# Where the last six scatters of list entries run in a mixture-of-experts kernel, and when slot 3's list is loaded

## The chip, the cores and the metric

The kernel runs on one core of one Trainium2 chip. The metric is the device time of one execution in microseconds. The kernel before took 495.93 us as the median of three runs (495.6 to 498.26 us).

The core has five engines, each with its own instruction queue: TensorE (PE in the profile: matmuls; PEld: its weight loads), VectorE (DVE), ScalarE (ACT), GpSimd (POOL) and SyncE (SP). They wait for each other through semaphores. SP issues the plain DMAs and POOL the indirect ones (gathers and scatters by a list of rows); both run on the core's 16 DMA engines.

## The reference

A windowed attention is followed by a mixture of experts, in which each token goes to one of eight experts. The part that matters here is the second:

```
logits = x @ w_gate                       # x: 3072 x 512, w_gate: 512 x 8
e_idx  = np.argmax(logits, axis=1)        # one expert for each token
gate_w = softmax(logits)[token, e_idx]
eom    = 1 / (1 + np.exp(-(x @ w_output_gate)))
for e in range(8):
    mask = e_idx == e
    h  = np.maximum(x[mask] @ w1[e], 0.0)         # 512 x 1024
    ye = h @ w2[e]                                # 1024 x 512
    out[mask] = gate_w[mask, None] * eom[mask, e, None] * ye
```

The attention has 4 batches of 768 tokens; x is its output.

## The kernel before

**Lists.** For each batch, `route` finds each token's expert and its place in that expert's list. The lists lie in DRAM (`l_dr`). An entry is 8 bytes: the token's row and its weight. A batch has 768 tokens, six for each of 128 partitions, so POOL writes its entries with six indirect DMAs of 128 entries each (line 629), each after a memset of one column of a small tile `gap` (line 628). These are the scatters. `route` is a generator; for the last batch `attention` hands out its last six steps as a list of functions, `scatters`, and each call issues one memset and one scatter.

**Slots.** The experts' work is cut into slots of 256 tokens of one expert. The first three (`EARLY = 3`: slots 0, 1 and 2) are filled from the first batches alone. Which expert and which part of its list slots 3 and up take is found by `rest_slots`, some twenty small steps on DVE, which need the last batch's counts. For a slot, `fetch_list` (line 872) reads the list's place into a register of SP, lets SP load the 256 entries (line 880) and makes this load wait for all scatters issued so far in the program; `fetch` lets POOL gather the 256 rows of x (line 893) into `xg`.

**A slot's work.** `take_x` transposes the gathered rows on TensorE (line 943), and ACT and DVE split them into a rounded part and a residue. The first product has eight steps (`first`, lines 980 to 982): 12 matmuls of 256 columns each into one of the four PSUM banks P, S, p, s in turn; ACT takes the rounded part of the result (`hh`, line 983), DVE the residue (`hl`, line 984). The second product has eight steps too (`second_block`, lines 1290 to 1292) of six matmuls of 512 columns, which accumulate in two further banks; step j needs `hh` and `hl` of step j. At the end DVE and ACT scale the result (lines 1319 and 1321), and POOL writes the rows to the output by an indirect DMA (line 1322).

**Weights.** SP loads weight tiles of 128x512 into a ring of raw tiles (line 923), and ACT (line 931) and DVE (line 932) split each into a rounded part and a residue, once the tile of the slot before is free. The weights of slots 1 and 2 are loaded by an own loop (`load_ahead`), called each time a raw tile is split (`split`).

**Order.** Up to the end of slot 1 the order on all engines is written out by hand: `attention` and then `full_with(1, ...)`, which is the function that is changed. It goes through slot 1's first product; after each step it takes up to three steps of `rest_slots`, splits up to one tile of weights and issues one scatter. Then come the eight steps of the second product, with `take_x` for slot 2 ahead of the third step; after a step, once the table of slots 3 and up is made, it calls `fetch_list(3)`; and it splits the remaining weights of slot 2. After it come the write of slot 1's rows, the gather for slot 3 and the load of slot 4's list. From slot 2 on (`run`) only POOL's order is fixed by hand; a planner orders the other engines.

Of the kernel before, what the change touches and what calls it, by code (L numbers as in the profile page):

```python
# [11 lines left out]
F32 = mybir.dt.float32  # L12
# [39 lines left out]
NF = F // P  # L52
SLOT = 256
EARLY = 3
# [212 lines left out]
def in_bank(ps, bank, shape, name):  # L267
    return ps.tile(shape, F32, name=name, tag=f"bank{BANKS.index(bank)}", bufs=1)
# [560 lines left out]
class Experts:  # L829
# [244 lines left out]
    def full_with(self, s, scatters, rest):  # L1074
        hidden = self.hidden()
        made = None
        for j in range(NF):
            self.first(j, hidden, None)
            self.free += 4 * (j % 4 == 3)
            for _ in range(REST):  # L1080
                made = made or next(rest, None)
            self.split(EARLY_V, "v")
            if scatters:
                scatters.pop(0)()
        yp = [in_bank(self.ps, "Vv"[t], [P, DM], f"yp{t}") for t in range(2)]
        for j in range(NF):
            if j == 2:
                self.take_x(2)
            self.second_block(j, yp, *hidden)
            self.free += 1  # L1090
            if not self.slots.get(EARLY):
                for _ in range(REST):
                    made = made or next(rest)
                if made:
                    self.add_slots(made[0])
                    self.fetch_list(EARLY, 2)
            self.split(-(-len(self.behind) // (NF - j)))
        self.write(s, yp)
        assert not self.behind and not scatters
        self.fetch(EARLY, 2)  # L1100
        self.fetch_list(EARLY + 1, 2)
        return made[1]
# [323 lines left out]
```

## Time and profile before

| what | value |
|---|---|
| median of three runs | 495.93 us |
| the profiled execution, its own time | 493.42 us |
| its span, from the first to the last instruction | 491.3 us |
| mean granted clock of TensorE | 0.99 |
| TensorE busy | 468.6 us (95% of the span) |
| DVE, ACT, POOL busy | 365.7, 315.4, 179.5 us (74%, 64%, 37%) |

The profile was taken from one execution. All times in it count from the first instruction. An engine is busy while it executes an instruction; in the timeline a number in brackets is the idle time before a row, with what ended it. PEclk is the clock that TensorE was granted, as a share of 2.4 GHz. The DMA share is the mean over the 16 DMA engines; it passes 1 in some stretches.

### The profile page before, as it was taken

What the parts mean: (1) busy time and instruction counts of PE and PEld (TensorE: products, weight loads), DVE (VectorE), ACT (ScalarE), POOL (GpSimd) and SP (SyncE); (2) the same over time, 40 slices, a digit from 0 to 9 for tenths busy, and PEclk for the clock granted to TensorE, in tenths of its full rate; (3) what the DMA queues carried; (4) which work ended last, traced back from release to release, by engine and by line L of the source; (5) the groups of instructions that cost most, each with busy time, mean ns of one, the idle gap of its engine ahead of it and who ended that gap; (6) DMA issues with size and microseconds to landing.
All of it is one profiled execution on the core that took longest, in us unless ns stands there. A gap on an engine that the chain in (4) does not pass through costs nothing. (4 is left out here: it accounts for less than half of the span.)

```text
span 491.3 us, 12041 instructions
## 1 busy us (share of the span) xinstructions
PE 468.6 (95%) x4060; PEld 379.8 (77%) x4060; DVE 365.7 (74%) x822; ACT 315.4 (64%) x647; POOL 179.5 (37%) x194
## 2 busy tenths in 40 slices
PE   9999999997699999799999999999999999999994
PEld 4757886875488776689888888888888888888873
DVE  4988899799388529695778878787878689879610
ACT  2586787986396336265676868686767579679500
POOL 2575784537574367603130021203122212303101
PEclk9999999999899999989999999999999999999998
DMA  9997997969194628829877485867675678874730
GB/s 240 218 189 174 280 224 188 264 126 249 53 333 139 193 86 296 328 80 355 264 223 267 138 291 160 288 191 273 179 270 187 220 240 282 314 239 139 242 143 13
DMA packets 109962, 105.33 MB, mean 214 GB/s; under 512 B 47929, under 2 KB 72891, under 8 KB 109884
## 3 DMA queue, kind: packets, MB, share of 16 engines
q1 hardware_dynamic: 104588, 91.78, 64.2%
q0 software_dynamic: 5296, 12.62, 7.0%
q8 instruction: 35, 0.57, 0.5%
q14 instruction: 43, 0.35, 0.2%
HBM read 93.08 MB, written 13.46 MB: 217 GB/s over the span
## 5 line engine op out<-in xcount | busy, mean ns | idle before, releaser
L932 DVE TENSOR_TENSOR w2l<-raw,w2h 128x512 fp32r<-128x512 f32 x101 | 70.5, 716 | 21.4 <-ACT w2h L931 20.2
L931 ACT ACTIVATE w2h<-raw 128x512 fp32r<-128x512 f32 x104 | 64.7, 630 | 26.8 <-PE yp L1292 19.3
L893 POOL DMA_INDIRECT xg<-x_dr,lst x30 | 35.9, 1195 | 124.3 <-PE xp L943 108.1
L932 DVE TENSOR_TENSOR w1l<-raw,w1h 128x512 fp32r<-128x512 f32 x99 | 66.2, 694 | 6.4 <-ACT w1h L931 2.9
L1290 PE MATMUL yp<-w2h,hh 128*128 128x512 f32 x176 | 70.5, 401 | 0.0
L1291 PE MATMUL yp<-w2l,hh 128*128 128x512 f32 x176 | 69.4, 394 | 0.0
L1292 PE MATMUL yp<-w2h,hl 128*128 128x512 f32 x176 | 68.7, 396 | 0.2
L1322 POOL DMA_INDIRECT out_dram<-y,lst x26 | 27.8, 1068 | 105.6 <-DVE y L1319 30.3
L931 ACT ACTIVATE w1h<-raw 128x512 fp32r<-128x512 f32 x104 | 62.1, 624 | 2.7 <-PE hp L969 1.5
L973 PE MATMUL hp<-xhl,w1h 128*128 128x512 f32 x216 | 62.1, 395 | 0.0
L478 POOL TENSOR_TENSOR pr<-pr,mn 128x960 f32<-128x960 f32 x24 | 43.7, 1824 | 27.1 <-DVE mn L473 10.4
L971 PEld LDWEIGHTS hp<-xhl,w1l 128*128 128x128 f32 x288 | 44.3, 189 | 5.9
L971 PE MATMUL hp<-xhl,w1l 128*128 128x256 f32 x288 | 46.1, 281 | 0.0
L983 ACT ACTIVATE hh<-hs 128x256 fp32r<-128x256 f32 x72 | 29.8, 413 | 17.8 <-DVE hs L976 14.2
L1292 PEld LDWEIGHTS yp<-w2h,hl 128*128 128x128 f32 x176 | 33.3, 190 | 8.1 <-DVE hl L1135 1.0
L984 DVE SCALAR_TENSOR_TENSOR hl<-hs,hh 128x256 fp32r<-128x256 f32 x72 | 30.3, 421 | 11.9 <-ACT hh L983 10.6
L1291 PEld LDWEIGHTS yp<-w2l,hh 128*128 128x128 f32 x176 | 33.5, 190 | 6.8
L1290 PEld LDWEIGHTS yp<-w2h,hh 128*128 128x128 f32 x176 | 33.4, 190 | 6.7
L973 PEld LDWEIGHTS hp<-xhl,w1h 128*128 128x128 f32 x216 | 35.8, 189 | 3.2
L976 DVE TENSOR_TENSOR hs<-hp,hs 128x256 f32<-128x256 f32 x72 | 30.3, 421 | 9.8 <-ACT hs L975 7.5
L975 ACT ACTIVATE hs<-hp 128x256 f32<-128x256 f32 x72 | 27.2, 378 | 13.9 <-PE hp L973 10.5
L466 DVE TENSOR_TENSOR pr<-sp,c_sb 128x480 f32<-128x480 f32 x48 | 28.9, 649 | 8.9 <-PE sp L456 5.6
(223 smaller groups left out, 962.0 us busy)
## 6 DMA issues: line engine op xcount, KB each, us to landing
raw<-in_moe_w_dram SPq DMA_DIRECT2D x224, 256.0 KB
raw_k<-in_k_dram SPq DMA_DIRECT2D x12, 512.0 KB
raw_q<-in_q_dram SPq DMA_DIRECT2D x12, 512.0 KB
x_dr<-xs SPq DMA_DIRECT2D x24, 256.0 KB
vw<-in_v_dram SPq DMA_DIRECT2D x44, 128.0 KB
vw<-in_v_dram SPq DMA_DIRECT2D x44, 64.0 KB
w1l<-in_moe_w_dram SPq DMA_DIRECT2D x8, 256.0 KB
w2l<-in_moe_w_dram SPq DMA_DIRECT2D x8, 256.0 KB
```

The lines of the kernel that those rows point to most:

```text
L478: nc.gpsimd.tensor_tensor(pr, pr, mns.pop(i).unsqueeze(2).to_broadcast([P, H, W]), ALU.subtract)
L893: nc.gpsimd.indirect_dma_start(out=self.xg[t], out_offset=None, in_=self.x_dr[0:rows, :], in_offset=bass.IndirectOffsetOnAxis(ap=self.list ...
L931: nc.scalar.activation(hi, raw, AF.Copy)
L932: (lo_by or nc.vector).tensor_tensor(lo, raw, hi.bitcast(F32), ALU.subtract)
L971: nc.tensor.matmul(hp[:, 0, :], lhsT=w_l[c], rhs=self.xh[:, c, :], start=False, stop=False)
L973: nc.tensor.matmul(hp, lhsT=w_h[c], rhs=self.xhl[:, c], start=False, stop=c == NC - 1)
L976: nc.vector.tensor_tensor(hs, hp[:, 0, :], hs, ALU.add)
L983: nc.scalar.activation(hh[:, j, :], hs, AF.Relu)
L984: nc.vector.scalar_tensor_tensor(hl[:, j, :], hs, 0.0, hh[:, j, :].bitcast(F32), ALU.max, ALU.subtract)
L1290: nc.tensor.matmul(y, lhsT=hh[:, j, tk], rhs=w_h, start=j == 0, stop=False)
L1291: nc.tensor.matmul(y, lhsT=hh[:, j, tk], rhs=w_l, start=False, stop=False)
L1292: nc.tensor.matmul(y, lhsT=hl[:, j, tk], rhs=w_h, start=False, stop=j == NF - 1)
```

## The change

The six scatters no longer stand in the loop over the first product. After that loop POOL copies one element column of the last step's residue (`hidden[1][:, NF - 1, 0:1]`) into the small tile `gap`, and so waits for DVE's last step of the first product. The six calls stand in the loop over the second product, one after each of its first six steps. `fetch_list(3)` is called once no scatter is left, that is in the sixth step, where it was called in the first step in which the table is made.

```diff
--- before.py
+++ after.py
@@ -1080,20 +1080,22 @@
             for _ in range(REST):
                 made = made or next(rest, None)
             self.split(EARLY_V, "v")
-            if scatters:
-                scatters.pop(0)()
+        self.tc.nc.gpsimd.tensor_copy(self.rt["gap"][:, 0:1], hidden[1][:, NF - 1, 0:1].bitcast(F32))
         yp = [in_bank(self.ps, "Vv"[t], [P, DM], f"yp{t}") for t in range(2)]
         for j in range(NF):
             if j == 2:
                 self.take_x(2)
             self.second_block(j, yp, *hidden)
             self.free += 1
+            if scatters:
+                scatters.pop(0)()
             if not self.slots.get(EARLY):
                 for _ in range(REST):
                     made = made or next(rest)
                 if made:
                     self.add_slots(made[0])
-                    self.fetch_list(EARLY, 2)
+            if not scatters and self.slots.get(EARLY) and EARLY not in self.lists:
+                self.fetch_list(EARLY, 2)
             self.split(-(-len(self.behind) // (NF - j)))
         self.write(s, yp)
         assert not self.behind and not scatters
```

## Rows read from the trace of the kernel before

**Rows 1.** Stretches: us; PE, PEld, DVE, ACT, POOL busy (instructions); PEclk; DMA share; GB/s
```profile
208.00:480.00 272.00, 271.83 (x1451) 228.99 (x1450) 207.98 (x404) 186.00 (x388) 54.18 (x47) 0.99 0.68 225
```

**Rows 2.** Stretches of 2 us, same columns
```profile
120.00:122.00 2.00, 1.78 (x43) 1.58 (x39) 1.86 (x9) 0.88 (x1) 1.77 (x3) 1.00 0.96 308
...
126.00:128.00 2.00, 0.35 (x3) 0.00 (x0) 0.00 (x0) 0.00 (x0) 1.78 (x4) 1.00 0.06 12
...
175.00:177.00 2.00, 2.00 (x13) 1.80 (x12) 1.03 (x5) 0.47 (x2) 1.48 (x3) 1.00 0.01 1
...
202.00:204.00 2.00, 1.46 (x11) 1.09 (x10) 0.98 (x4) 0.00 (x0) 1.78 (x4) 1.00 1.04 402
...
208.00:210.00 2.00, 2.00 (x7) 1.52 (x6) 1.86 (x8) 2.00 (x7) 0.00 (x0) 0.59 0.03 8
...
212.00:214.00 2.00, 2.00 (x15) 1.74 (x14) 1.97 (x6) 1.40 (x4) 0.00 (x0) 1.00 0.00 0
```

**Rows 3.** Timeline of POOL: start, us, engine line op out<-in xcount [idle before <-releaser]
```profile
120.04 0.98 POOL L629 DMA_INDIRECT l_dr<-pair,posi  x1 [0.16 <-DVE den L511]
...
126.39 0.96 POOL L629 DMA_INDIRECT l_dr<-pair,posi  x1 [0.19 <-issue]
...
171.76 1.05 POOL L629 DMA_INDIRECT l_dr<-pair,posi  x1 [1.06 <-DMA raw<-in_moe_w_dram]
...
175.69 0.97 POOL L629 DMA_INDIRECT l_dr<-pair,posi  x1 [0.19 <-issue]
...
198.62 0.98 POOL L629 DMA_INDIRECT l_dr<-pair,posi  x1 [0.19 <-issue]
...
202.46 1.40 POOL L629 DMA_INDIRECT l_dr<-pair,posi  x1 [0.19 <-issue]
...
205.44 0.97 POOL L629 DMA_INDIRECT l_dr<-pair,posi  x1 [0.19 <-issue]
...
223.74 1.00 POOL L1322 DMA_INDIRECT out_dram<-y,lst  x1 [17.33 <-DVE y L1319]
```

**Rows 4.** Timeline of TensorE (PE), slot 1's two products
```profile
192.28 0.28 PE L981 MATMUL hp<-xhl,w1h 128*128 128x256 f32 x1
...
202.68 0.28 PE L980 MATMUL hp<-xhl,w1h 128*128 128x256 f32 x1
...
207.80 0.40 PE L1290 MATMUL yp<-w2h,hh 128*128 128x512 f32 x1
...
212.15 1.03 PE L943 MATMUL xp<-id_sb,xg 128*128 128x128 f32 x8
...
213.72 0.39 PE L1290 MATMUL yp<-w2h,hh 128*128 128x512 f32 x1
...
221.20 0.64 PE L980 MATMUL hp<-xhl,w1h 128*128 128x256 f32 x4
```

**Rows 5.** Timeline of ACT
```profile
128.71 0.60 ACT L335 ACTIVATE qt<-qtr 128x512 f32<-128x512 f32 x1 [7.83 <-remote]
...
204.63 0.38 ACT L983 ACTIVATE hh<-hp 128x256 fp32r<-128x256 f32 x1 [5.62 <-PE hp L982]
...
226.86 0.62 ACT L931 ACTIVATE w1h<-raw 128x512 fp32r<-128x512 f32 x1
```

**Rows 6.** Timeline of DVE, slot 1's first product
```profile
200.94 0.42 DVE L984 SCALAR_TENSOR_TENSOR hl<-hp,hh 128x256 fp32r<-128x256 f32 x1
...
202.33 0.69 DVE L932 TENSOR_TENSOR w1l<-raw,w1h 128x512 fp32r<-128x512 f32 x1
...
208.04 0.42 DVE L984 SCALAR_TENSOR_TENSOR hl<-hp,hh 128x256 fp32r<-128x256 f32 x1 [1.33 <-ACT hh L983]
...
211.54 0.42 DVE L984 SCALAR_TENSOR_TENSOR hl<-hp,hh 128x256 fp32r<-128x256 f32 x1
```

**Rows 7.** Timeline of the DMA queue of SP (SPq)
```profile
213.06 2.57 SPq L880 DMA_DIRECT2D lst<-l_dr  x3
...
216.48 12.09 SPq L923 DMA_DIRECT2D raw<-in_moe_w_dram  x16
```

## Prediction

> **What bounds the kernel now.** I read four views in this order. First the busy time by stretch: from 208 us to 480 us TensorE is busy for 271.83 of 272 us [rows 1]. So whatever TensorE wins before 208 us it keeps, unless a later stretch falls out of that state; and whatever other engines win is worth nothing there. The change lies in slot 1 (191.8 to 221.2 us), so the second view is the same table in steps of 2 us: the end of slot 1's first product is the exception. TensorE works 1.46 of 2 us from 202, and from 208 to 210 its granted clock is 0.59, that is mostly at the lower of its two levels (1.2 instead of 2.4 GHz), before it is 1.00 again at 212 [rows 2].
>
> The third view is the timeline of TensorE. The first product is 96 matmuls at a pitch of 0.12 us; the 88th starts on time at 202.68, and the remaining eight need until the second product's first at 207.80 [rows 4]. ACT, which evacuates each step, has the same hole: it waits 5.62 us until 204.63 [rows 5]. No engine has a long instruction there. The fourth view, POOL's timeline, shows what does run: the six scatters of the last batch, 198.62 to 206.41, back to back [rows 3].
>
> Do the scatters make the hole? Two other bursts in this trace speak to it. Six scatters in a row (120.04 to 126.39) begin with DMA at 0.96 and end at 127.35 [rows 2, 3]; ACT stands still for 7.83 us until 128.71 [rows 5], and at 126 TensorE is busy 0.35 of 2 us although DMA has fallen to 0.06 [rows 2]. But four scatters (171.76 to 175.69) with DMA at 0.01 leave TensorE busy 2.00 of 2 us [rows 2, 3]. I read: a run of scatters that begins while DMA is loaded holds back what TensorE reports and issues, and the hold lasts as long as the run; begun in quiet, it does not. At 202 to 204 DMA is at 1.04, at 212 to 214 at 0.00 [rows 2]. The name of the mechanism I leave open.
>
> **The change part by part.**
>
> Taken out of the first product: six pairs of a small memset and a scatter. Ideal end of that product: 202.68 plus eight pitches of 0.12 and one handover of 0.11, 203.75. It is 207.80 now: 4.05 us. The lowered clock that follows the idle time costs the twelve matmuls from 207.80 to 212.15 (4.35 us) the difference to the pitch of 0.227 that holds from 213.72 to 221.20 (33 matmuls in 7.48 us) [rows 4]: 4.35 less 12 x 0.227 is 1.63 us. Together **5.7 us**, if the hold goes.
>
> Added: one copy of 128x1 on POOL that waits for DVE's last step of the first product. Nearest price: the small memsets beside it, 0.1 us (estimate from the 0.3 us between a scatter's end and the next one's start, which holds one); nothing below zero. Queued behind it on POOL are the six scatters, then the two writes of slot 1's rows, for which nothing on the chip waits, and slot 3's gathers, which TensorE wants a whole slot later; POOL idles 17.33 us before the first of these [rows 3], so that idle time covers copy and scatters. Without that cover the writes would start later by the whole burst.
>
> When does the copy's wait end? DVE has its own backlog in the first product: the fourth step's residue starts at 200.94, the sixth's at 208.04, the eighth's at 211.54, the last two 1.75 us apart each [rows 6]. Freed of the hold, four such steps from 200.94 give 208 us, ending 208.4. So the burst runs from about 208.6, not from the end of TensorE's first product. A scatter comes every 1.36 us (198.62 to 205.44, five intervals) [rows 3]: done near 216.8. Beside DVE's split of two inputs one took 1.40 instead of about 0.97 us (202.46, split from 202.33) [rows 3, 6]; if all six do, the burst ends 2.6 us later, near 219.4. I take 218. The program order says "one to a step", but nothing ties POOL to TensorE's steps: they run as a burst after the copy.
>
> The Trainium skill ("GPSIMD Engine Reference", section 1, Specifications) says that POOL shares its SBUF interfaces with VectorE and contends with its instructions of two SBUF inputs. That speaks against the new place, which is full of such splits; the one row at 202.46 agrees. By the rule alone all six would be slow, the lists would be 1.4 us later than I take, and the gain about 1 us smaller.
>
> Inside the second product TensorE needs nothing from the scatters. It needs DVE's residue of each step (the eighth at 208, used near 214) and slot 2's gathered rows, landed long ago. So a burst in quiet DMA costs it **0**; the bound from the other side is the first rival.
>
> Moved: slot 3's list. SP issues it at 213.06 now, when the slot table is ready; the lists of slots 4 and 5 and the first of sixteen weight loads of slot 3 (216.48) stand behind it [rows 7]. No load of slots 1 and 2 is left by then (DMA 0.00 at 212 [rows 2]), so moving past their splits costs nothing. But the list waits for the last scatter to land: at 219, not 213, so slot 3's first load goes out near 222.5 instead of 216.48. ACT wants that tile at 226.86 now [rows 5], 10.4 us after its issue; in the changed kernel near 221.2, before it is even sent. ACT would wait some 2 us (222.5, plus at least 0.65 for 256 KB at the 402 GB/s of [rows 2], less 221.2), with the next steps' evacuations queued behind it on ACT and DVE. Four banks hold four steps of the product, so part of this never reaches TensorE. Bounds: 0 (the banks, or the planner putting evacuations ahead) and 4 us (burst slow, nothing covered). I take **1.2 us**, nearer to the covered end because the banks are certain.
>
> Sum: 5.7 - 1.2 = 4.5 us. Against the profiled execution's own 493.42 us (span 491.3 and 2.1 around it) that is 488.9. The median of the runs is 495.93, 2.5 us above the profiled one; the saving is a time and not a ratio, so I take the same 4.5 from it: **491.4**.
>
> **Rivals.**
>
> *The hold moves along.* The burst holds TensorE's reports in the second product too (the six-scatter burst did so with DMA at 0.06 [rows 2]). TensorE itself can go on: in the first product it ran 34 matmuls from 198.62 to 202.68 before it stopped [rows 4]; 34 at 0.227 are 7.7 us of second product. The Trainium skill ("TensorE: Matmul & The Clock Gate", the section on the array's architecture) gives TensorE a queue of 64 instructions; with a weight load to each matmul that would be 32 matmuls, and the trace's 34 agree. So the second product is nearly covered, but DVE and ACT are not: released near 218, DVE then has five splits (0.69 each [rows 6]), one output and one residue (taken as long as a split, an estimate) ahead of slot 2's fifth step, 4.8 us, so that step starts at 222.8 instead of 221.2. With the 1.2 us of the late loads the gain is 5.7 - 1.6 - 1.2 = 2.9; if TensorE's own work is out at 216.3 (208.6 and 7.7) and it misses most of the time to 218 as well, 1.4 less. 493.0 to 494.4, in the middle 493.7. For it: that burst. Against it: the quiet burst of four.
>
> *The hole is not the scatters'.* It belongs to loads and stores that fill DMA (1.04 at 202 [rows 2]) and stays. Then the copy waits until 212, the lists come 9 us later, which the 10.4 us of slack just cover: 495.9. For it: the hole ends with the traffic (0.03 at 208). Against it: DMA at 0.06 in the other hole, with TensorE as idle [rows 2].
>
> *Slower: both holds.* The hole stays and the burst adds its own, from 212 to 221, over the evacuation of slot 2's rows, whose transposes run at 212.15. They are then ready near 224 and TensorE stands from 221.2: 2.8 us, and 1.6 more if the clock falls again as it did at 208. 499.5. It decides if the burst starts before those rows are evacuated.
>
> *The change does not take effect*, since the planner orders SP and the later slots: it may put slot 3's loads ahead of its list. That would remove my 1.2 us (490.2) or, by loading DMA beside the burst, bring the first rival; its chance lies in those two.
>
> **How the numbers follow.** Forecast (490.2 to 493.2): 0.56. The hold moves along: 0.15, about half of it on either side of the bound. The hole stays: 0.17. Slower: 0.12. A measurement of this kernel can tell about 0.5%, 2.5 us, from no change. Faster by more: 0.56 + 0.07; within: 0.08 + 0.17; slower: 0.12. The range goes from 5.7 us with the 0.4 us between the median and the lowest run (489.8) to 497.0, which leaves out the slower rival.
>
> **What would show it.** Right: slot 1's second product starts near 203.8 and its clock stays 1.00; six scatters run after the last residue of the first product, in quiet DMA, with ACT following TensorE at once; slot 2 starts near 215.5; TensorE busy without a gap from there. The 1.2 us would be a gap in slot 2's first product ended by ACT or DVE that waits for a load of slot 3. Wrong: the hole is still there without scatters; or ACT stands for 5 us and more during the second product; or SP's first load of slot 3 comes later than 226.

## The result, and the profile after

The changed kernel took **490.13 us** (median of 13 runs) beside 495.79 us for the kernel before (13 runs): a ratio of 0.989, 95% interval 0.9865 to 0.9916. 491.4 us had been forecast. The profiled execution took 489.96 us, its span is 487.8 us.

Stretches of the changed kernel (columns as in [rows 1]):

```profile
202.00:204.00 2.00, 2.00 (x19) 2.00 (x19) 1.90 (x12) 1.41 (x5) 0.00 (x0) 1.00 1.04 409
206.00:208.00 2.00, 2.00 (x12) 1.70 (x11) 1.96 (x10) 1.55 (x4) 0.00 (x0) 1.00 1.05 405
...
214.00:216.00 2.00, 2.00 (x10) 1.66 (x9) 2.00 (x4) 1.10 (x2) 1.75 (x4) 1.00 0.01 1
...
206.00:478.00 272.00, 271.83 (x1460) 229.21 (x1459) 208.27 (x409) 185.05 (x384) 64.12 (x61) 1.00 0.69 229
```

TensorE is busy 2.00 of 2 us where it had 1.46 [rows 2], its granted clock stays at 1.00, and DMA is as loaded as before there (1.04 and 1.05). Timeline of TensorE, slot 1:

```profile
194.79 0.28 PE L981 MATMUL hp<-xhl,w1h 128*128 128x256 f32 x1
...
206.25 0.40 PE L1292 MATMUL yp<-w2h,hh 128*128 128x512 f32 x1
...
218.05 0.64 PE L980 MATMUL hp<-xhl,w1h 128*128 128x256 f32 x4
```

Against [rows 4]: from the second matmul of slot 1 to its second product it takes 11.46 us (before: 192.28 to 207.80, 15.52), that is 4.06 less; from there to slot 2 it takes 11.80 (before 13.40), 1.60 less. Together 5.66 us, and the medians are 5.66 us apart. The two spans differ by 3.5 only, mainly because slot 1 starts 2.5 us later in this execution (194.79 against 192.28): what stands ahead of it took longer, and the change doesn't touch that. The remaining 0.35 us are won behind slot 2's start.

Timeline of POOL, and then of the DMA queue of SP:

```profile
210.97 0.19 POOL L1083 COPY gap<-hl 128x1 f32<-128x1 f32 x1 [10.16 <-DVE at_rest L822]
...
211.35 1.45 POOL L629 DMA_INDIRECT l_dr<-pair,posi  x1 [0.15 <-issue]
...
214.87 0.96 POOL L629 DMA_INDIRECT l_dr<-pair,posi  x1 [0.19 <-issue]
...
219.68 0.96 POOL L629 DMA_INDIRECT l_dr<-pair,posi  x1 [0.19 <-issue]
```

```profile
222.35 2.36 SPq L880 DMA_DIRECT2D lst<-l_dr  x3
224.97 11.21 SPq L923 DMA_DIRECT2D raw<-in_moe_w_dram  x16
```

The burst stands where it was expected, 211.35 to 220.64 (the last scatter's start plus its 0.96); SP's lists and loads come 9.3 and 8.5 us later than in [rows 7], 2.5 of which are the attention's. ACT in slot 2's first product:

```profile
224.01 0.39 ACT L983 ACTIVATE hh<-hp 128x256 fp32r<-128x256 f32 x1 [0.46 <-PE hp L982]
228.00 0.63 ACT L931 ACTIVATE w1h<-raw 128x512 fp32r<-128x512 f32 x1 [3.61 <-DMA raw<-in_moe_w_dram]
...
230.19 0.37 ACT L983 ACTIVATE hh<-hp 128x256 fp32r<-128x256 f32 x1
```

ACT waits 3.61 us for the late load, and the evacuation of slot 2's fifth step stands behind it until 230.19. TensorE is nevertheless busy throughout (271.83 of 272 us above).

### The profile page after: what moved, and what is told of

The parts are those of the page before. It is cut to its first block, busy times and chain, and to the rows that moved or that the text cites. A ratio compares the mean times of both kernels' runs of the same rounds, so it can differ in the third digit from the quotient of the medians.

```text
span 487.8 us, 12036 instructions
## 1 busy us (share of the span) xinstructions
PE 467.2 (96%) x4060; PEld 379.8 (78%) x4060; DVE 364.7 (75%) x822; ACT 316.0 (65%) x647; POOL 181.7 (37%) x195
## 5 line engine op out<-in xcount | busy, mean ns | idle before, releaser
L893 POOL DMA_INDIRECT xg<-x_dr,lst x30 | 37.3, 1243 | 128.7 <-PE xp L943 111.4
```

What stands on the lines that cost most here:

```text
L893: nc.gpsimd.indirect_dma_start(out=self.xg[t], out_offset=None, in_=self.x_dr[0:rows, :], in_offset=bass.IndirectOffsetOnAxis(ap=self.list ...
```

## The experiments

Each run is compared with the kernel before on the same chip. There were four chips, of two kinds: on chips 8 and 12 the kernel before took 496.67 and 495.37 us, on chips 2 and 0 it took 481.04 and 481.2 (the result above, with 495.79, is of the first kind). This turned out to be a result of its own, and which kind it was is told each time. "Hold" below means that engines stand although what they wait for is done: the profile ends ACT's wait with TensorE's work long after that work was over, or TensorE itself issues only now and then.

It is the copy that moves the scatters: POOL has nothing else to do between their old place and the new one (it idles 10.16 us ahead of the copy), so without it they would come no later than before. The changed kernel without the copy was not run.

**Six small gathers in the old place** (chip 8). The scatters stay behind the copy.

```diff
             self.split(EARLY_V, "v")
+            if j < 6:
+                self.tc.nc.gpsimd.memset(self.rt["gap"][:, 6 + j:7 + j], 0.0)
+                self.tc.nc.gpsimd.indirect_dma_start(out=seen[:, j, :], in_=self.x_dr[0:ROWS0, :], ...)
```

> The changed kernel, and in slot 1's first product six small gathers where the scatters stood (128 rows of 8 bytes each, out of the x rows in DRAM into SBUF), back to back on POOL with the same memsets between them; the scatters stay behind the copy. The gathered entries are used by nothing. Order on all other engines as in the changed kernel. Theory A1 (any run of six indirect DMAs under a loaded DMA holds the reports): the hole is back, 4 us and the half clock, 494.5 to 496.5. Theory A2 (it is the writing of list entries to DRAM that holds): no hole, 489.5 to 490.8. In between would be a hold of the gathers that is shorter than the 4 us of matmuls that TensorE has ahead: late reports without a hole.

Measured: 498.79 us, ratio 1.0046 (1.0014 to 1.0078). Two stretches, and the row of ACT:

```profile
206.00:208.00 2.00, 0.47 (x3) 0.27 (x2) 0.24 (x1) 0.00 (x0) 1.81 (x3) 1.00 1.05 397
...
210.00:212.00 2.00, 1.49 (x6) 1.17 (x6) 0.73 (x5) 1.15 (x4) 0.00 (x0) 0.55 0.18 58
```

```profile
210.85 0.38 ACT L983 ACTIVATE hh<-hp 128x256 fp32r<-128x256 f32 x1 [7.88 <-PE hp L982]
```

The hole is back, with the low clock behind it, though nothing is written to the lists there; with ACT standing for 7.88 us it is longer than in the kernel before, and the time is 2.3 us above the range of theory A1. So it is a run of indirect DMAs on POOL that makes it, and not only one of scatters. In this kernel as in the one before, the run is longer than six: the two writes of slot 0's rows come directly ahead of it (here at 199.21 and 200.53, before at 195.99 and 197.31).

**A copy ahead of each scatter in the old place** (chip 8), so that each waits for the residue of its own step.

```diff
-        self.tc.nc.gpsimd.tensor_copy(self.rt["gap"][:, 0:1], hidden[1][:, NF - 1, 0:1].bitcast(F32))
 # in the loop over the first product, behind self.split:
+            if scatters:
+                self.tc.nc.gpsimd.tensor_copy(self.rt["gap"][:, 0:1], hidden[1][:, j, 0:1].bitcast(F32))
+                scatters.pop(0)()
```

> The six scatters stand in slot 1's first product again, as before the change, but each behind a copy on POOL that waits for DVE's residue of its step (steps one to six). On TensorE, ACT, DVE and SP the order of instructions is that of the kernel before. Theory A (a run of scatters under a loaded DMA holds back what the engines report, and the hold grows with the run): a scatter now can't go before the report of its own step has come through, so the run stops itself; each report is late by one scatter or two (1.4 to 2.8 us), the 34 matmuls that TensorE can run ahead (4 us) cover that: the hole of 4.05 us is under 1 us and 490.2 to 492 us. Theory B (scatters in the first product cost what they cost there, whatever their spacing): the hole stays near 4 us with the half clock behind it, 495 to 496.5 us.

Measured: 491.44 us, 0.9868 (0.9827 to 0.991). The worst stretch, the longest wait of ACT, and POOL's fourth scatter with the copy behind it:

```profile
208.00:210.00 2.00, 1.25 (x8) 1.10 (x8) 1.17 (x8) 1.59 (x4) 0.79 (x3) 1.00 1.06 401
```

```profile
208.41 0.38 ACT L983 ACTIVATE hh<-hp 128x256 fp32r<-128x256 f32 x1 [5.03 <-PE hp L982]
```

```profile
207.60 0.98 POOL L629 DMA_INDIRECT l_dr<-pair,posi  x1 [0.16 <-issue]
209.38 0.18 POOL L1084 COPY gap<-hl 128x1 f32<-128x1 f32 x1 [0.81 <-DVE counts L793]
```

The first scatters (203.09, 204.49, 205.85) came 1.36 to 1.40 us apart, and ACT stood for 5.03 us. TensorE lost 0.95 us (0.75 here and 0.20 in the two microseconds before) and kept its clock. The time and the lost work are as theory A said; its mechanism isn't shown. The one copy that had to wait, the fifth (0.81 us, until 209.38), began to do so at 208.57, when ACT was already free again (208.41). What stands ahead of ACT's release is a longer step on POOL: the fourth copy took 0.57 us, and the fourth scatter came 1.75 us after the third. The kernel is nearly as good as the changed one, with scatters, list and loads in their early place.

**Slot 3's loads beside the burst** (chip 8).

```diff
                     self.add_slots(made[0])
+                    for i in range(NF):
+                        self.load_w(1, EARLY, i, self.place(1, EARLY, i))
```

(`place` is the ring's index as `fetch_w` works it out; `fetch_w` then only splits these tiles.)

> The changed kernel, but the first eight weight loads of slot 3 (256 KB each) go out as soon as the slot table is there, ahead of the lists, and so run beside the six scatters of the second product. Theory A (loaded DMA is what makes a run of scatters hold): the burst starts in quiet and is overtaken by loads some 2 us later; from there the reports of TensorE come late until the burst ends near 220, ACT and DVE stand for 4 us or more, and TensorE, which can run 34 matmuls of 0.23 us ahead, stands 1 to 3 us around slot 2's start: 491.5 to 494. Theory C (the place is what counts: beside the second product a burst is harmless, loaded or not): reports in time, TensorE busy throughout, 489.5 to 490.5; the wait of ACT for slot 3's first weights (3.61 us) is gone in both, worth nothing on TensorE.

Measured: 490.56 us, 0.9875 (0.9828 to 0.9922), and the same stretch from slot 1 to slot 3 as the changed kernel. The burst ran from 211.50 to 220.79:

```profile
214.00:216.00 2.00, 2.00 (x11) 1.65 (x10) 2.00 (x4) 0.96 (x2) 1.81 (x4) 1.00 0.92 273
216.00:218.00 2.00, 2.00 (x11) 1.65 (x10) 2.00 (x4) 0.94 (x2) 1.65 (x3) 1.00 0.97 232
```

With DMA at 0.92 to 0.97 in these four microseconds ACT never waited over 0.96 us during the burst. Loaded DMA beside a run of scatters doesn't by itself make a hold. That ACT no longer waits 3.61 us for slot 3's first weights is worth nothing.

**The burst nine microseconds later** (chip 8): the copy waits for DVE's last split of slot 2's weights.

```diff
-        self.tc.nc.gpsimd.tensor_copy(self.rt["gap"][:, 0:1], hidden[1][:, NF - 1, 0:1].bitcast(F32))
 # behind the loop over the second product, where the six calls and fetch_list(EARLY, 2) stand now:
+        self.tc.nc.gpsimd.tensor_copy(self.rt["gap"][:, 0:1], self.wt[2][1][NF - 1][:, 0:1].bitcast(F32))
```

> The changed kernel with the copy on POOL waiting not for the last residue of the first product (210.5) but for DVE's last split of slot 2's weights (219.7): the burst, the writes of slot 1's rows, the list and slot 3's loads come some 8 to 9 us later. Theory D (the late list is free only because slot 2's first product has banks for all the steps that wait, so that the slack is some 7 us and then goes over to TensorE): the first load of slot 3 comes near 233 and lands near 236, after the second product of slot 2 wants its fifth step (235): TensorE stands 1 to 5 us in slot 2's second product or at slot 3's start, 491.5 to 495.5. Theory E (the slack is larger than 9 us, since the planner puts the evacuations ahead of the splits): 489.5 to 490.8 and no idle time of TensorE over 0.3 us.

Measured: 496.68 us, 1.0 (0.9971 to 1.003): the whole gain is gone. The burst ran from 220.42 to 227.71, one scatter each 1.27 us, beside slot 2's first product:

```profile
224.00:226.00 2.00, 2.00 (x15) 1.83 (x14) 0.00 (x0) 0.00 (x0) 1.62 (x4) 1.00 0.03 1
...
230.00:232.00 2.00, 0.64 (x5) 0.61 (x5) 0.00 (x0) 0.07 (x1) 0.29 (x1) 1.00 0.54 176
232.00:234.00 2.00, 2.00 (x12) 1.81 (x12) 1.51 (x4) 1.25 (x4) 0.42 (x1) 0.74 0.30 89
```

```profile
231.93 0.94 ACT L983 ACTIVATE hh<-hp 128x256 fp32r<-128x256 f32 x3 [5.39 <-PE hp L982]
```

Not the lateness that was to be tested, but a hold, with DMA at 0.03: 5.39 us for ACT, and TensorE idle for 1.36 of 2 us with the clock low after it. The two writes of slot 1's rows follow at the same pace (228.02 and 229.31), so this run has eight DMAs and ends at 230.29; ACT is free at 231.93. **The reading that a run begun in quiet DMA holds nothing falls here.** The lateness shows too: at slot 3's start TensorE waited 1.33 us for DVE's part of slot 3's rows.

**What is it, then?** Left were the pace of the run (1.36, 1.38 and 1.27 us from one DMA to the next where it held, 1.67 where it didn't) and what TensorE runs beside it (first products where it held, second products where it didn't). The next runs were to part these, but their chip had no hold at all.

**The kernel before with a pause behind each scatter** (chip 2, and once more on chip 0).

```diff
             if scatters:
                 scatters.pop(0)()
+                self.tc.nc.gpsimd.memset(pause, 0.0)        # 128x384, 0.44 us
```

> The kernel before, with a fill of 128x384 on POOL (estimate 0.4 us, from the 0.49 us that a fill of 128x512 took) behind each of the last batch's six scatters in slot 1's first product: one comes every 1.7 us or so instead of every 1.36, as beside DVE's splits in the changed kernel (1.67). All other engines as in the kernel before. Theory P (POOL's pace is what counts: in the changed kernel the scatters were harmless because DVE slowed them): no hole, 490 to 491.5 us. Theory F (what counts is what TensorE runs beside it: 256-column matmuls at a pitch of 0.12 us in a first product, 512-column ones at 0.23 us in a second product; the second holds nothing): the run holds the reports in spite of its pace, it ends 2 us later than before, near 208 to 209, and the hole is as long or longer, 4 to 6 us: 495.5 to 498.

Measured: 481.1 us beside 481.04 for the kernel before, 0.9998 (0.997 to 1.0026); on chip 0 1.0008 (0.9975 to 1.004). No hole:

```profile
194.00:196.00 2.00, 2.00 (x19) 2.00 (x19) 1.86 (x13) 1.02 (x3) 1.84 (x4) 1.00 1.05 417
196.00:198.00 2.00, 2.00 (x17) 1.91 (x16) 2.00 (x10) 1.28 (x4) 1.83 (x4) 1.00 1.04 397
```

That decides nothing on the pace: the kernel before, without pauses, was as fast on these chips (481.04 and 481.2 us). So the changed kernel went onto such a chip too.

**The changed kernel on a chip of the other kind** (chip 0).

> The changed kernel once more, as it is. On the chip of the last four runs the kernel before took 481 us, 15 us less than on the chips of the runs before them, and there six scatters in a row beside slot 1's first product left TensorE busy throughout. If the gain is the hold and nothing else (theory H), it belongs to the chip: where the kernel before takes 481 us and its trace shows no hold, the changed kernel is within 1.5 us of it; where the kernel before takes 495 us and more, it gains 5 to 6.5 us again. If the gain had another part (theory G: the order of evacuations and splits in slot 2, which the planner changed), some of it is there on either chip.

Measured: 480.8 us, ratio **0.9998 (0.9971 to 1.0024)**. There the change is worth nothing. The stretches of TensorE from about slot 1's second product on, TensorE's first matmul of slot 1, and ACT behind the six-scatter burst of the attention:

```profile
194.00:466.00 272.00, 271.83 (x1461) 229.27 (x1460) 208.47 (x412) 185.12 (x385) 64.51 (x61) 1.00 0.69 231
```

```profile
182.63 0.68 PE L980 MATMUL hp<-xhl,w1h 128*128 128x256 f32 x1
```

```profile
119.84 0.60 ACT L335 ACTIVATE qt<-qtr 128x512 f32<-128x512 f32 x1 [0.77 <-PE qtr L415]
```

From slot 1's first matmul to the end of the span it takes 293.7 us here (476.3 less 182.63) and 293.5 us in the profile of the result (487.8 less 194.27, the row before the one shown above): the same. The 11.6 us between the two executions all lie ahead of slot 1: 3.2 of them ahead of the attention's six-scatter burst (it begins at 117.83 here, at 121.06 there), the other 8.4 from its start on. ACT waits 0.77 us behind that burst on this chip and 7.83 in [rows 5]. So theory H held: the gain is the hold, and the hold belongs to the chip.

**Four more on chips without a hold.** They were meant for the other kind. *Three scatters in the old place, three behind the copy* (chip 2): 482.89 us, 1.003 (0.9996 to 1.0063); TensorE busy 20.00 of 20 us from 180 on; on what three scatters cost where there is a hold it says nothing.

> The changed kernel, but three of the six scatters stay in slot 1's first product as before the change, and three follow behind the copy. Theory A in its weaker form (the hold lasts as long as the run): the two writes of slot 0's rows and three scatters end near 205 in this kernel's time, 4 us after the first late report; TensorE's 34 matmuls ahead cover that: a hole under 1 us, 490 to 491.5. Theory N (any scatter in the first product costs its share, 4.05 us for six): a hole of 2 us and a low clock behind it, 492 to 494.

*Twelve gathers more in slots 4 and 6* (chip 2): 483.1 us, 1.0055 (1.0017 to 1.0092); TensorE busy in every stretch from slot 4 to slot 6; where the 2 us come from is open.

> The changed kernel with two runs more of six small gathers (128 rows of 8 bytes, as in the run with gathers), whose entries nothing uses: one behind the last residue of slot 4's first product, so beside its second product, and one behind the first residue of slot 6's first product. DMA is loaded at both places (0.7 to 1.0). Theory F: no idle time of TensorE in slot 4's second product, a hole of 2 to 6 us in slot 6's first product and its end, with ACT standing for 5 us or more: 493 to 497. Theory A (loaded DMA is enough): reports are late in both; a hole at both places, or at none if TensorE's 34 matmuls ahead cover it, but then ACT stands for 4 us and more in slot 4's second product too: 493 to 499. Neither: 489.5 to 490.8, and the hold belongs to something that only slots 1 and 2 and the attention have.

*The attention's scatters in groups behind POOL's products* (chip 2), by moving their steps in the written order: 487.85 us, 1.0167 (1.0098 to 1.0237), a miss. Where nothing is held, the products behind the scatters only come later: TensorE is busy 4.31 of 10 us from 130 to 140, where the changed kernel had 8.69 (chip 0). What it would do on the other kind of chip is open. The same order with the pauses and the twelve gathers together (chip 0), meant to test four places in one kernel, took 489.06 us, 1.0156 (1.0083 to 1.0228), and met no hold either.

> The changed kernel with the twelve scatters of the first two batches moved on POOL too: not eleven of them nearly in a row (112.8 to 128.4 us) but three, three, two, two and two, each group behind one of the five POOL products that need what the other engines report. Only POOL's order differs. In the changed kernel TensorE is busy 1.26 and 1.68 of 4 us from 124 and 128, and from 130 to 136 its clock is 0.5 to 0.66. Theory A in its weaker form (a run holds the reports as long as it lasts, and work that needs reports between the scatters ends it): that hole of 5 us and the low clock behind it (6 us at half) go for the most part; later products of POOL stand behind scatters instead. 482 to 488 us. Rival (the hole is the attention's own order, its loads or POOL's products): 489 to 492.

**Late and paced** (chip 12, where the kernel before took 495.37 us): the run with the late copy, and a pause behind each scatter.

```diff
+        pause = self.const.tile([P, 384], F32, name="pause", tag="pause")
         while scatters:
             scatters.pop(0)()
+            self.tc.nc.gpsimd.memset(pause, 0.0)
```

> The run with the late copy (behind DVE's last split of slot 2's weights) with a fill of 128x384 on POOL behind each of the six scatters, so one comes every 1.6 us instead of 1.27, beside slot 2's first product and in quiet DMA; list and loads of slot 3 come 11 us later than in the changed kernel, and 2 us later than in that run. On a chip where the kernel before takes 481 us there is no hold, and the time is that of the lateness alone: theory D (the slack of the late list ends within these 11 us; in the run with the late copy DVE's evacuation of slot 3's rows, behind the late gathers, ended a wait of TensorE of 1.33 us at slot 3's start): TensorE stands 2 to 5 us at slot 3's start, 2 to 6 us slower than the kernel before; theory E (slack beyond that): within 1 us of it. On a chip where the kernel before takes 495 us and more: theory P (pace counts): no hole in slot 2's first product, where that run had 1.47 of 4 us from 228 and a low clock behind it; theory F (what TensorE runs beside it): that hole again, 2 us later.

Measured: 497.36 us, 1.004 (1.0013 to 1.0067). ACT in the attention, and in slot 2's first product beside the burst (221.60 to 230.60, one scatter each 1.61 us), then three stretches:

```profile
133.22 0.60 ACT L335 ACTIVATE qt<-qtr 128x512 f32<-128x512 f32 x1 [7.92 <-PE qtr L415]
...
227.79 0.38 ACT L983 ACTIVATE hh<-hp 128x256 fp32r<-128x256 f32 x1 [1.97 <-PE hp L982]
229.23 0.38 ACT L983 ACTIVATE hh<-hp 128x256 fp32r<-128x256 f32 x1 [1.06 <-PE hp L982]
```

```profile
226.00:228.00 2.00, 2.00 (x18) 1.96 (x17) 0.28 (x1) 0.21 (x1) 1.71 (x5) 1.00 0.02 1
...
242.00:244.00 2.00, 0.29 (x3) 0.06 (x1) 1.40 (x3) 0.55 (x1) 0.00 (x0) 1.00 0.95 337
244.00:246.00 2.00, 0.87 (x6) 0.64 (x6) 0.69 (x1) 1.67 (x4) 0.85 (x1) 1.00 1.05 404
```

In one execution the unpaced run of the attention (121.72 to 129.03, one scatter each 1.27 us) holds: TensorE gets only one to five matmuls through at a time from 123.84 to 130.35, and ACT stands for 7.92 us. The paced run beside slot 2's first product holds nothing: TensorE is busy throughout from 220 to 232, and ACT follows each step (the 1.97 us contain four matmuls of the second product, from 225.24, that stand between two steps). In that same place the unpaced run held ACT for 5.39 us. So it is theory P and not F: **in this place the pace of the run counts.** This rests on one pair of kernels, on two chips that both hold. A pause also puts another POOL instruction between the scatters; whether the time or the instruction does it is open. In the changed kernel there is only the time (DVE slows the scatters), but a second product beside it, and no experiment put an unpaced burst there.

The pace isn't all of it. The execution of the kernel before that shows two holds has two unpaced bursts without one: five scatters (111.81 to 118.02, 1.26 to 1.44 us apart), during which ACT waited 0.99 us at most, and the four from 171.76 (1.27 to 1.36 apart). Those that held had six DMAs or more, counting the writes next to them. No run varied the number on a chip that holds, so what it does is open.

And here the late list has its price: at slot 3's start TensorE is busy 0.29, 0.87 and (from 246) 0.56 of 2 us, and the clock falls behind it. The rows show first a wait of TensorE for slot 3's gathered rows (1.81 us), then for DVE's part of those rows (2.45 us):

```profile
244.11 0.87 PE L943 MATMUL xp<-id_sb,xg 128*128 128x128 f32 x6 [1.81 <-DMA xg<-x_dr,lst]
...
247.44 0.79 PE L969 MATMUL hp<-xhl,w1h 128*128 128x512 f32 x1 [2.45 <-DVE xhl L946]
```

No run beat the changed kernel. Pauses behind the attention's scatters, on a chip that holds, were not tried.

## Why the prediction was right, and where not

**The bound, and the two terms of the gain**: right to a few hundredths. The hole was put at 4.05 us and gave 4.06; the half clock at 1.63 and gave 1.60.

**The hold belongs to the scatters, not to the load**: right. The first product now runs under the same DMA (1.04) without a hole, and six gathers in the place bring it back. The rival that the hole stays is out.

**"Begun while DMA is loaded it holds, begun in quiet it does not"**: the step that was wrong, though the sum didn't suffer. The late copy gave a hold at DMA 0.03; the early loads gave none at 0.95. The row that misled was read for too much: 0.01 is the DMA share from 175 to 177, when the four scatters of [rows 3] were nearly over. When they began it was 0.76. The same trace:

```profile
171.00:173.00 2.00, 2.00 (x12) 0.54 (x11) 0.48 (x3) 0.00 (x0) 1.16 (x2) 1.00 0.76 255
```

```profile
172.62 0.64 PE L537 MATMUL lp<-xT,wg_sb 128*32 128x256 f32 x8
...
175.02 0.52 PE L547 MATMUL lt<-c_sb,ls 128*128 128x16 f32 x4
```

```profile
173.39 0.38 ACT L335 ACTIVATE ls<-lp 128x256 f32<-128x256 f32 x1 [4.44 <-PE lp L537]
175.57 0.20 ACT L335 ACTIVATE lg<-lt 128x32 f32<-128x32 f32 x1 [1.80 <-issue]
```

That the four held nothing was right: ACT takes both results within 0.13 us of TensorE's end (173.26 and 175.54). But they were no quiet run: begun at 0.76 and holding nothing, they speak against the rule and not for it. "As long as the run" wasn't exact either: in the kernel before ACT was free at 204.63, 1.8 us ahead of the run's end (and stood once more, 2.09 us, until 207.62), in the late copy 1.6 us behind it.

That six scatters beside the second product cost TensorE 0 came true, but not for the reason given. What the runs offer instead is that there they take longer: four of the six took 1.44 to 1.50 us beside DVE's splits, and the run's pace was 1.67 us. The prediction had this as a cost; that it makes the place harmless fits the run that was late and paced, and isn't shown for a second product. The Trainium skill ("GPSIMD Engine Reference", section 1, Specifications) has POOL contend with VectorE's instructions of two SBUF inputs. The trace agrees for all six: the four long ones ran beside such splits, the other two (214.87 and 219.68, 0.96 us each) began beside DVE instructions that read PSUM. So the burst's end lies between the two sums that were made.

**The copy's time and the burst's**: foreseen were 208.4 for the end of its wait and 216.8 to 219.4 for the end of the burst; less the 2.5 us by which slot 1 started later they came at 208.5 and 218.1 (218 was taken). The upper one was 0.4 us too long, since the pace of 1.36 already contains one scatter of 1.40 us; nothing hung on that.

**The late list, 1.2 us**: the term that was mis-sized; it measured 0. First load and wait came as foreseen (222.5 after the same correction; ACT waits 3.61 us, not some 2). But the four banks don't hold "part" of what waits: when the wait begins (224.4) the first four steps are evacuated, so the banks take all four that are left. The second product then has the first four steps to work on, and first uses the fifth step's evacuation behind them:

```profile
235.18 0.48 PE L1292 MATMUL yp<-w2h,hh 128*128 128x512 f32 x1
```

ACT gave it at 230.19, 5 us ahead. Of the 1.3 us between forecast and result 1.2 are this term. Two runs then measured where the slack ends: with the list 6.6 us later than in the changed kernel, counted from slot 2's start, TensorE lost 1.33 us at slot 3's start (the hold had also delayed slot 2's products there), with 8.7 us 4.3 us and a low clock. What TensorE waited for there was not the weights, which the prediction followed, but the rows that are gathered by the same list, and their evacuation.

**The rivals**: that the hold moves along could have come true, as the late copy shows for a first product; what kept it away here is open between the pace and the place. The range's lower end is 0.07 us off, as the lowest run lay 0.33 us below the median and not 0.4. The planner left the list ahead of the loads, and the other order is worth nothing.

**What no step had**: that the gain depends on the chip. The rows of one trace can't show it.

## What to carry to other kernels

When one engine's wait is ended by another that had long been done, look at what POOL issues at that time: runs of six and more small indirect DMAs, reads or writes, held the other engines on some chips. Two ways out gained here: the place of the changed kernel, where each comes a little slower, and a copy ahead of each that waits for what the other engines report. A quiet place by itself didn't help. Read the DMA share where a run begins, and the row of the engine that waits, before calling a run harmless. Price a late load by the steps that free buffers can take and by when their results are first used, and follow everything that hangs on it; and measure a gain of a per cent on more than one chip.

## What the hardware showed that was not expected

The same kernel takes 495 to 497 us on two of the chips and 481 on two others. Of the two executions that were compared, 8.4 of the 11.6 us come from the start of a run of six scatters in the attention on: on the first kind ACT stands for 7.8 us there, on the second for 0.77. In slot 1 the change removes another 5.7 us of the difference. Where the hold exists, runs of six and more at 1.27 to 1.40 us to an indirect DMA on average made it, with DMA at 0.03 as at 1.05; bursts of four and five at that pace showed none; and six at 1.61 (beside matmuls of 256 columns, DMA at 0.02) and at 1.67 (beside 512 columns, DMA at 0.01 as at 0.97) made none. After TensorE had stood, its granted clock was 0.50 to 0.60 in whole stretches of 2 us. Why the number in a run matters, if it does, what holds the reports back inside the chip, and what sets the two kinds of chip apart, no run here shows.
